# Reordering and splitting in a linear-attention and gated-MLP kernel: half-size crossbar transposes, a fifth output buffer, maxima split on VectorE, the tail's projection per batch, more tasks a step

## The chip, the cores and the metric

The kernel runs on one core of a Trainium2 chip. The metric is the device time of one execution in microseconds (us). Before the change the first three runs took 294.79, 297.31 and 300.43 us; with a fourth run beside the changed kernel the median is 296.06 us. Engines: PE is TensorE (PEld its weight loads), DVE is VectorE, ACT is ScalarE, POOL is GpSimd, SP is SyncE, which here only issues DMAs. Runs are called fast or slow by their time against the fastest of the same kernel. The profile of before was taken in a run of 301.7 us, state slow; that of the changed kernel in a run of 311.41 us, state fast.

## The reference

Two stages. The first is attention with a feature map for 8 batches, 8 heads, 576 tokens, head size 64; the second is a gated MLP that mixes tokens.

```python
def phi(x):
    proj = einsum('bhsd,df->bhsf', x, w_phi)
    proj = proj - max(abs(proj), axis=-1, keepdims=True)
    return concatenate([exp(proj), exp(-proj)], axis=-1)
q_p, k_p = phi(q), phi(k)
kv  = einsum('bhsf,bhsd->bhfd', k_p, v);   z = sum(k_p, axis=2)
out = einsum('bhsf,bhfd->bhsd', q_p, kv) / (einsum('bhsf,bhf->bhs', q_p, z)[..., None] + 1e-6)
x = out with heads side by side                        # 8 x 576 x 512
h = maximum(x @ w_in, 0);  u, v = halves of h          # 512 columns each
v_n = (v - mean(v)) / sqrt(var(v) + 1e-6)
v_s = einsum('ts,bsd->btd', w_spatial, v_n) + b_spatial
y = (u * v_s) @ w_out
```

## The kernel before

576 tokens are four blocks of 128 and a tail of 64. The attention runs in units: 32 units of two heads of one batch (four a batch), and four tail units, which each hold the 64-token tails of two batches. Each loop step starts the projections of one unit, while older units are in later phases. The second stage of a batch is a list of tasks: v (a projection, whose rows are normalised on GpSimd, `vn`), u (the other half), s (mixing of tokens, reads `vn`), o (the last matrix). Each step hands out tasks from a queue against a credit.

```python
def cross(b):                                    # both transposes of a whole batch, two steps ahead
    d = st[b]
    for x in ("k", "q"):
        d[x + "T"] = ld.tile([P, 2 * H, P], BF16, tag=x + "T_b", name=x + "T_b", bufs=2)
        pin(nc.sync.dma_start_transpose)(out=d[x + "T"], in_=d[x].rearrange("p h x -> p (h x)"))

def r_queries(u):                                # maxima of the queries, in two bf16 parts
    m, early = mhl[u["i"] % NM], u["i"] < EARLY
    pq = u["pq"]
    mq = pq[0][:, 0, 0:H] if early else small.tile([P, H], FP32, tag="mq", name="mq")
    for par in range(2):
        nc.vector.tensor_reduce(out=mq[:, 4 * par:4 * par + 4], in_=pq[par], axis=AX.X, op=ALU.max,
                                apply_absolute_value=True)
    eng = nc.vector if early else nc.gpsimd      # ... the split itself
    # [cut]
    eng.tensor_copy(out=m[:, :, 0:4], in_=mq)
    eng.tensor_tensor(out=m[:, :, 4:8], in0=mq, in1=m[:, :, 0:4], op=ALU.subtract)

def b_tasks(b):
    g, bl = b // 2, b % 2
    alone = g in SPLIT                           # SPLIT = (0,): batches 0 and 1 are done singly
    bls = [bl] if alone else [0, 1]
    tail = alone or bl == 1
    ts = []
    if tail: ts.append((mm, lambda: b_v_tail(g, bls)))
    ts += [(mm, lambda j=j: b_v(b, j)) for j in range(NB)]
    ts.append((0.0, lambda: b_ln(b)))            # normalises v of this batch on GpSimd
    # [cut]
    ts += [(mm, lambda dc=dc: b_u(b, dc)) for dc in range(KC)]
    if tail:                                     # s and o of BOTH batches of the pair
        ts.append((mm * len(bls) / 2, lambda: b_u_tail(g, bls)))
        for x in bls: ts += [(ms, lambda dc=dc, x=x: b_s(2 * g + x, dc)) for dc in range(KC)]
        ts.append((ms * len(bls) / 2, lambda: b_s_tail(g, bls)))
        for x in bls: ts += [(mm, lambda j=j, x=x: b_o(2 * g + x, j)) for j in range(NB)]
        ts.insert(len(ts) - 2, (mm, lambda: b_o_tail(g, bls)))
    return ts

RATE = 3.35                                      # us of tasks a step
def fill(share):                                 # called four times a step
    credit[0] = min(credit[0] + RATE * share, CAP)
    while queue and credit[0] >= queue[0][0] / 2:
        cost, task = queue.pop(0); task(); credit[0] -= cost
```

`a_scale` of a tail unit scales the tail's values for both batches on GpSimd (`vst`); `tail_num` and `tail_x_t` are the tail's attention and its transposes. The chain from the maxima is DVE (maxima), GpSimd (split `mhl`; VectorE before unit 5), PE (a transpose), DVE (copy to `mT`), PE (features `pf` of the next step). PE's instructions are kept in program order from step 8 on, so a PE wait holds all later work.

Of the kernel before, what the change touches and what calls it, by code (L numbers as in the profile page):

```python
# [16 lines left out]
def kernel(  # L17
# [15 lines left out]
    nc = tc.nc  # L33
# [39 lines left out]
    def pin(start):  # L73
        return lambda *a, **kw: tc.keep_in_program_order(start(*a, **kw))
# [40 lines left out]
        for i in range(2):  # L115
            pin(eng.dma_start)(out=gs[g][x][i * TL:(i + 1) * TL], in_=tail_ap(t, 2 * g + i))

    def cross(b):
        d = st[b]
        for x in ("k", "q"):  # L120
            d[x + "T"] = ld.tile([P, 2 * H, P], BF16, tag=x + "T_b", name=x + "T_b", bufs=2)
            pin(nc.sync.dma_start_transpose)(out=d[x + "T"], in_=d[x].rearrange("p h x -> p (h x)"))


    wphi_f = cpool.tile([P, F], FP32)
# [2 lines left out]
    alloc(0)  # L128
    first = {}
    for x, t in (("k", k), ("q", q)):  # L130
        first[x] = s2.tile([P, 2, NB * D], FP32, tag="ob", name="first", bufs=4)
        pin(nc.sync.dma_start)(out=first[x], in_=main_ap(t, 0, 0, 2))
    ident = cpool.tile([P, P], BF16)
    make_identity(nc, ident)
# [46 lines left out]
    w_out_bf = cpool.tile([P, KC, DM], BF16)  # L181
    wsp = s2.tile([P, NB, T0], BF16, tag="vn", name="wsp", bufs=2)
    wspr = cpool.tile([P, NB, TL], BF16)
    wspt = ld.tile([TL, S], BF16, tag="kT_b", name="wspt", bufs=2)
    bsp_row = ld.tile([P, S], FP32, tag="qT_b", name="bsp_row", bufs=2)
    nc.sync.dma_start(out=bsp_row[TL:TL + 1, :], in_=moe_b_spatial)
    nc.sync.dma_start(out=bsp_row[0:1, :], in_=moe_b_spatial)

# [35 lines left out]

    def a_transpose(u):
        src = st[u["b"]] if u["pair"] else gs[u["g"]]
        if "kT" in src:
            for x in ("kT", "qT"):
                u[x] = src[x][:, 4 * u["pj"]:4 * u["pj"] + 4, :] if u["pair"] else src[x]
            return  # L230
        for x, copy in (("k", nc.vector.tensor_copy if u["i"] < EK else nc.scalar.copy), ("q", nc.vector.tensor_copy)):
            pt = psum.tile([P, 4, P], BF16, tag="bank", name="pt")
            for j in range(4):
                if u["pair"]:
                    blk = src[x][:, 2 * u["pj"] + j // 2, (j % 2) * P:(j % 2 + 1) * P]
                else:
                    blk = src[x][:, 2 * j:2 * j + 2, :]
                transpose(out=pt[:, j, :], in_=blk, identity=ident)
            u[x + "T"] = a1.tile([P, 4, P], BF16, tag=x + "T", name=x + "T", bufs=2 if x == "k" else 4)
            copy(out=u[x + "T"], in_=pt)  # L240
# [51 lines left out]
                                 bias=0.0, scale=sc)  # L292

    def r_queries(u):
        m, early = mhl[u["i"] % NM], u["i"] < EARLY
        pq = u["pq"]
        mq = pq[0][:, 0, 0:H] if early else small.tile([P, H], FP32, tag="mq", name="mq")
        for par in range(2):
            nc.vector.tensor_reduce(out=mq[:, 4 * par:4 * par + 4], in_=pq[par], axis=AX.X, op=ALU.max,  # L299
                                    apply_absolute_value=True)  # L300
        eng = nc.vector if early else nc.gpsimd
        m = m.rearrange("p (par n) -> p par n", par=2)
        mq = mq.rearrange("p (par n) -> p par n", par=2)
        eng.tensor_copy(out=m[:, :, 0:4], in_=mq)
        eng.tensor_tensor(out=m[:, :, 4:8], in0=mq, in1=m[:, :, 0:4], op=ALU.subtract)

    def a_scale(u):
        em = small.tile([P, 2, H], FP32, tag="em" if u["pair"] else "em_t", name="em", bufs=3 if u["pair"] else 1)
# [146 lines left out]
    def b_v_tail(g, bls):  # L455
        d = gs[g]
        r = slice(bls[0] * TL, (bls[-1] + 1) * TL)
        vr = s2.tile([P, HALF], BF16, tag="vr", name="vr", bufs=5)
        stats = small.tile([P, 6], FP32, tag="stats", name="stats")
        mv = small.tile([P, 1, 2], FP32, tag="mv_t", name="mv_t")  # L460
        v_mm(lambda kc: d["xTt"][:, kc, r], vr, r, stats, mv[:, 0, :])
        rstd = root(mv, r, 1)
        for bl in bls:
            r = slice(bl * TL, (bl + 1) * TL)
            normalize(vnt[g % 2][r, bl, :], vr[r], rstd[r, 0, :])

    def b_u(b, dc):
        d = st[b]
        pu = psum.tile([P, T0], FP32, tag="bank", name="pu")
        for kc in range(KC):  # L470
            matmul(out=pu, lhsT=w_in_bf[:, kc, dc * P:(dc + 1) * P], rhs=d["xT"][:, kc, :],
                             start=(kc == 0), stop=(kc == KC - 1))
        nc.scalar.activation(out=d["uT"][:, dc, :], in_=pu, func=AF.Relu, bias=0.0, scale=1.0)
# [38 lines left out]
    def o_mm(lhs, r):  # L512
        po = psum.tile([P, DM], FP32, tag="bank", name="po")
        for dc in range(KC):
            matmul(out=po[r], lhsT=lhs(dc), rhs=w_out_bf[:, dc, :], start=(dc == 0), stop=(dc == KC - 1))
        ob = s2.tile([P, DM], FP32, tag="ob", name="ob", bufs=4)
        (nc.scalar.copy if drain[0] else nc.vector.tensor_copy)(out=ob[r], in_=po[r])  # L517
        return ob

# [30 lines left out]
    def b_tasks(b):  # L550

        g, bl = b // 2, b % 2
        alone = g in SPLIT
        bls = [bl] if alone else [0, 1]
        tail = alone or bl == 1
        mm = KC * T0 / 2400.0
        ms = (KC + 1) * T0 / 2400.0
        ts = []
        if tail:
            ts.append((mm, lambda: b_v_tail(g, bls)))  # L560
        ts += [(mm, lambda j=j: b_v(b, j)) for j in range(NB)]
        ts.append((0.0, lambda: b_ln(b)))
        if b == 0:
            ts += [(0.3, lambda i=i: transpose_spatial(i)) for i in range(NB + 1)]
        ts += [(mm, lambda dc=dc: b_u(b, dc)) for dc in range(KC)]
        if tail:
            ts.append((mm * len(bls) / 2, lambda: b_u_tail(g, bls)))
            for x in bls:
                ts += [(ms, lambda dc=dc, x=x: b_s(2 * g + x, dc)) for dc in range(KC)]
            ts.append((ms * len(bls) / 2, lambda: b_s_tail(g, bls)))  # L570
            for x in bls:
                ts += [(mm, lambda j=j, x=x: b_o(2 * g + x, j)) for j in range(NB)]
            ts.insert(len(ts) - 2, (mm, lambda: b_o_tail(g, bls)))
        return ts

    RATE = 3.35
    CAP = 2.5
    LAGS = dict(next=-1, maxima=1, features=2, sums=2, attention=3, out=4)
    FIRST = dict(next=-1, maxima=1, features=2, sums=2, attention=3, out=3)
# [58 lines left out]
            run("maxima", a_max_t)  # L638

    def finish_batch(u, f):  # L640
        g, bl = u["g"], u["b"] % 2
        if g in SPLIT:
            f(g, [bl])
        elif bl == 1:
            f(g, [0, 1])


    AT, AB, XP = 4, 5, 2
# [2 lines left out]
    def at(i, f, *a):  # L651
        io.setdefault(i, []).append(lambda: f(*a))
# [11 lines left out]
    for u in units:  # L664
        if not u["pair"] and u["g"] > 0:
            at(u["i"] - AT, load_tail, "k", u["g"])
            at(u["i"] - AT + 1, load_tail, "q", u["g"])
            at(u["i"] - AT + 1, load_tail, "v", u["g"])
        if u["pair"] and u["pj"] == 0 and u["b"] > 1:
            at(u["i"] - AB, load, "k", u["b"])  # L670
            at(u["i"] - AB + 1, load, "q", u["b"])
            at(u["i"] - AB + 1, load_v, u["b"], nc.sync)
            if u["b"] >= XB:
                at(u["i"] - XP, cross, u["b"])
    for i in range(NU + 4):
        step(i)
        for f in io.get(i, []):
# [34 lines left out]
```

## Time and profile before

| | before |
|---|---|
| median of 4 runs | 296.06 us |
| span of the profiled run (state slow) | 299.8 us |
| busy PE / DVE / ACT / POOL | 253.3 / 216.9 / 215.3 / 180.4 us |
| start of step 8 to start of step 35 | 50.9 to 240.7 us |
| last matmul | 295.2 us |

I cut the trace by steps: a step is the stretch from one unit's first key matmul (pk) on PE to that of the next. The windows view gives the busy time of each engine (us, number of instructions) in a stretch; here the steps 8 to 34 of the kernel before, and what follows:

```profile
50.90:240.70 189.80, 166.01 (x2286) 102.52 (x2284) 147.62 (x357) 151.80 (x358) 126.90 (x233) 0.96 0.87 136
240.70:295.20 54.50, 54.42 (x512) 29.42 (x508) 31.91 (x73) 24.79 (x47) 15.64 (x29) 1.00 0.22 75
```

The order is PE, PEld, DVE, ACT, POOL, then the granted clock, the DMA share and GB/s. In the first stretch PE, DVE and ACT are all within 43 us of the full 189.8; in the second PE alone is full. The prediction below shows the waits.

### The profile page before, as it was taken

The page shows a single profiled execution, that of the slowest core. Times are in us where ns is not written, and L with a number is a line of the kernel's source. Part 1 is how long each engine was busy: PE and PEld are TensorE (multiplying, and loading weights), DVE is VectorE, ACT ScalarE, POOL GpSimd, SP SyncE. Part 2 cuts the span into 40 slices and gives each one's busy share as a digit, 9 for nine tenths or more (in the row PEclk, how much of TensorE's full clock was granted, in tenths as well). Part 3 has the DMA queues.
Part 4 walks back from the last instruction along what each step waited for, and adds up shares of the span by engine and source line. Part 5 has one row for each costly group of instructions (what it writes and reads, how often), then busy time and mean ns, then how long its engine had stood idle before and what let it go on. Part 6 is the DMA issues. An engine that isn't in the chain of part 4 may idle for free.

```text
span 299.8 us, 8368 instructions
## 1 busy us (share of the span) xinstructions
PE 253.3 (84%) x3270; PEld 155.7 (52%) x3270; DVE 216.9 (72%) x538; ACT 215.3 (72%) x488; POOL 180.4 (60%) x320
## 2 busy tenths in 40 slices
PE   3059988989897989869699999819999999999993
PEld 1037666666553546535456567414555656645451
DVE  6277998877998569678686899819779787855520
ACT  7547999898589778839998888607999965067033
POOL 8239988589436696365959973923398850038400
PEclk9999999999999899979899999978999999999998
DMA  7979999942869199979941999899910011520026
GB/s 178 212 145 130 209 241 200 160 142 33 115 179 137 40 204 143 152 208 224 134 97 37 203 150 127 215 281 224 144 21 18 20 20 65 175 81 2 0 105 210
DMA packets 81706, 40.32 MB, mean 134 GB/s; under 512 B 50242, under 2 KB 77058, under 8 KB 81668
## 3 DMA queue, kind: packets, MB, share of 16 engines
q1 hardware_dynamic: 54180, 28.32, 43.4%
q0 software_dynamic: 27328, 11.41, 35.0%
q8 instruction: 25, 0.41, 0.5%
q14 instruction: 13, 0.11, 0.1%
q10 hardware_dynamic: 160, 0.07, 0.1%
HBM read 32.85 MB, written 9.44 MB: 141 GB/s over the span
## 4 chain that ended last, share of the span: by engine, by line
PE 50%; ACT 19%; DMA 10%; DVE 9%; POOL 7%; issue 3%; SPq 0%; DVEq 0%; POOLq 0%; ACTq 0%
PE ps L62 11%; PE pv L62 10%; ACT qf L277 10%; PE po L62 9%; PE pf L62 5%; ACT kf L291 5%; PE pu L62 5%; DMA out_dram<-ob 4%; DMA q_tl<-in_q_dram 4%; PE pn L62 3%; PE pt L62 3%; DVE stats L421 2%; POOL vn L435 2%; DMA qT_b<-q_bf 2%; PE pk L62 2%
## 5 line engine op out<-in xcount | busy, mean ns | idle before, releaser
L277 ACT ACTIVATE qf<-pf 128x512 bf16<-128x512 f32 x144 | 75.2, 631 | 32.8 <-PE pf L62 32.8
L315 POOL TENSOR_TENSOR vs<-v_f,em 128x512 bf16<-128x512 f32 x64 | 65.9, 1043 | 36.9 <-ACT em L310 30.8
L291 ACT ACTIVATE kf<-pk 128x512 bf16<-128x512 f32 x144 | 79.4, 664 | 8.4 <-DVE mk L286 8.3
L286 DVE TENSOR_REDUCE mk<-pk 128x4 f32<-128x512 f32 x72 | 46.4, 684 | 13.0 <-PE pk L62 12.4
L299 DVE TENSOR_REDUCE mq<-pq 128x4 f32<-128x512 f32 x62 | 40.7, 681 | 0.3 <-PE pq L62 0.3
L62 PE MATMUL ps<-w_spT,vn 128*128 128x512 bf16 (+1 forms) x256 | 38.8, 287 | 1.7 <-POOL vn L435 0.9
L421 DVE BATCH_NORM_STATS2 stats<-vr 128x6 f32<-128x512 bf16 (+1 forms) x37 | 25.0, 685 | 11.2 <-ACT vr L420 11.2
L62 PE MATMUL pv<-w_in_bf,xT 128*128 128x512 bf16 x128 | 33.0, 398 | 0.0
L62 PE MATMUL pu<-xT,w_in_bf 128*128 128x512 bf16 x128 | 32.0, 385 | 0.7 <-DVE mq L299 0.5
L495 DVE TENSOR_TENSOR uT<-ps,uT 128x512 bf16<-128x512 f32 x32 | 22.0, 687 | 14.6 <-PE ps L62 12.7
L420 ACT ACTIVATE vr<-pv 128x512 bf16<-128x512 f32 (+1 forms) x37 | 22.7, 654 | 13.1 <-PE pv L62 12.8
L62 PE MATMUL po<-w_out_bf,uT 128*128 128x512 bf16 x128 | 32.0, 388 | 0.0
L62 PE MATMUL pv<-vs,kf 128*128 128x66 bf16 x512 | 26.1, 200 | 3.3 <-DVE ob L517 3.3
L517 DVE COPY ob<-po 128x512 f32<-128x512 f32 (+1 forms) x28 | 19.0, 686 | 13.5 <-DMA out_dram<-ob 10.4
L62 PEld LDWEIGHTS <-qf 128*128 128x128 bf16 (+1 forms) x640 | 23.8, 101 | 9.7 <-issue 2.4
L62 PEld LDWEIGHTS <-kf 128*128 128x128 bf16 x640 | 24.7, 101 | 7.7 <-issue 4.9
L62 PE MATMUL pn<-kv,qf 128*128 128x66 bf16 (+1 forms) x640 | 26.0, 195 | 2.1 <-ACT qf L277 1.9
L62 PE MATMUL pf<-mT,sel 64*128 64x128 bf16 x288 | 16.9, 232 | 11.5 <-DVE mT L337 10.6
L360 DVE TENSOR_TENSOR x<-pn,rc 128x256 bf16<-128x256 f32 x64 | 24.9, 417 | 0.3
L330 POOL TENSOR_TENSOR vst<-v_tl,em 64x512 bf16<-64x512 f32 x16 | 16.4, 1038 | 13.9 <-ACT em L310 13.7
L435 POOL TENSOR_SCALAR vn<-vr,rs 128x512 bf16<-128x512 bf16 x32 | 24.2, 768 | 0.7
L62 PEld LDWEIGHTS <-vn 128*128 128x128 bf16 x256 | 16.2, 98 | 13.9 <-POOL vn L435 1.8
(106 smaller groups left out, 450.1 us busy)
## 6 DMA issues: line engine op xcount, KB each, us to landing
v_f<-in_v_dram SPq DMA_DIRECT2D x8, 1024.0 KB, 10.5
out_dram<-ob SPq DMA_DIRECT2D x32, 256.0 KB, 2.5
k_bf<-in_k_dram POOLq DMA_DIRECT2D x7, 512.0 KB, 7.1
q_bf<-in_q_dram POOLq DMA_DIRECT2D x7, 512.0 KB, 7.8
v_tl<-in_v_dram SPq DMA_DIRECT2D x8, 128.0 KB, 6.5
w_in_bf<-in_moe_w_in_dram POOLq DMA_DIRECT2D x2, 512.0 KB, 7.9
out_dram<-ob SPq DMA_DIRECT2D x8, 128.0 KB, 2.4
k_tl<-in_k_dram POOLq DMA_DIRECT2D x8, 64.0 KB, 6.0
```

Source lines behind the costliest of these rows:

```text
L62: r = f(*a, **kw)
L277: nc.scalar.activation(out=qf[:, s, 4 * par:4 * par + 4, :], in_=u["pf"][par], func=AF.Exp, bias=0.0, scale=sc)
L286: nc.vector.tensor_reduce(out=mk[:, par, :], in_=u["pk"][par], axis=AX.X, op=ALU.max, apply_absolute_value=True)
L291: nc.scalar.activation(out=u["kf"][:, s, 4 * par:4 * par + 4, :], in_=u["pk"][par], func=AF.Exp, bias=0.0, scale=sc)
L299: nc.vector.tensor_reduce(out=mq[:, 4 * par:4 * par + 4], in_=pq[par], axis=AX.X, op=ALU.max, apply_absolute_value=True)
L315: nc.gpsimd.tensor_tensor(out=vs[:, s, :, 0:D], in0=st[u["b"]]["v"][:, pj * H:(pj + 1) * H, :], in1=em[:, s, :].unsqueeze(2).to_broadcast( ...
L360: nc.vector.tensor_tensor(out=x, in0=pn[r, :, 0:D], in1=rc[r].to_broadcast([n, 4, D]), op=ALU.mult)
L420: nc.scalar.activation(out=dst[r], in_=pv[r], func=AF.Relu, bias=0.0, scale=1.0)
L421: nc.vector.bn_stats(out=stats[r], in_=dst[r])
L435: nc.gpsimd.tensor_scalar(out=dst, in0=src, scalar1=rs[:, 0:1], scalar2=rs[:, 1:2], op0=ALU.mult, op1=ALU.add)
L495: nc.vector.tensor_tensor(out=d["uT"][:, dc, :], in0=ps, in1=d["uT"][:, dc, :], op=ALU.mult)
L517: (nc.scalar.copy if drain[0] else nc.vector.tensor_copy)(out=ob[r], in_=po[r])
```

## The change

The intent: take away PE's waits for DMAs and for output buffers, take the hop to GpSimd out of the maxima's chain, finish each batch before the next one comes, and leave less work for the end, where only PE is busy.

```diff
-    def cross(b):
+    def cross(b, x, part):                      # half a tensor at a time
+        t = ld.tile([P, H, P], BF16, tag=x + "T_b", name=x + "T_b", bufs=4)
+        st[b].setdefault(x + "T", {})[part] = t
+        pin(nc.sync.dma_start_transpose)(out=t, in_=st[b][x][:, 4 * part:4 * part + 4].rearrange("p h x -> p (h x)"))
 ...
-        mq = pq[0][:, 0, 0:H] if early else small.tile([P, H], FP32, tag="mq", name="mq")
+        mq = pq[0][:, 0, 0:H]                   # always in PSUM
 ...
-        eng.tensor_copy(...); eng.tensor_tensor(...)       # GpSimd from unit 5 on
+        nc.vector.tensor_copy(...); nc.vector.tensor_tensor(...)
 ...
-        ob = s2.tile([P, DM], FP32, tag="ob", name="ob", bufs=4)
+        ob = s2.tile([P, DM], FP32, tag="ob", name="ob", bufs=5)
 ...  in b_tasks
-        if tail:
-            ts.append((mm, lambda: b_v_tail(g, bls)))
+        ts = [(mm, lambda: b_v_tail(g, [bl]))]
 ...
-            for x in bls:
-                ts += [(ms, lambda dc=dc, x=x: b_s(2 * g + x, dc)) for dc in range(KC)]
+        ts += [(ms, lambda dc=dc: b_s(b, dc)) for dc in range(KC)]
 ...  (o likewise)
-    RATE = 3.35
+    RATE = 3.75
 ...  in finish_batch (the tail's attention and transposes)
-        if g in SPLIT: f(g, [bl])
-        elif bl == 1: f(g, [0, 1])
+        f(u["g"], [u["b"] % 2])
 ...  when the transposes are issued
-                at(u["i"] - XP, cross, u["b"])
+                for n, (x, part) in enumerate((("k", 0), ("q", 0), ("k", 1), ("q", 1))):
+                    at(u["i"] - XP - 1 + n, cross, u["b"], x, part)
```

More of the change, by code (lines that the diff above doesn't have):

```diff
@@ L116, in load_tail @@
             pin(eng.dma_start)(out=gs[g][x][i * TL:(i + 1) * TL], in_=tail_ap(t, 2 * g + i))
-    def cross(b):
-        d = st[b]
-        for x in ("k", "q"):
-            d[x + "T"] = ld.tile([P, 2 * H, P], BF16, tag=x + "T_b", name=x + "T_b", bufs=2)
-            pin(nc.sync.dma_start_transpose)(out=d[x + "T"], in_=d[x].rearrange("p h x -> p (h x)"))
+    def cross(b, x, part):
+        t = ld.tile([P, H, P], BF16, tag=x + "T_b", name=x + "T_b", bufs=4)
+        st[b].setdefault(x + "T", {})[part] = t
+        pin(nc.sync.dma_start_transpose)(out=t, in_=st[b][x][:, 4 * part:4 * part + 4].rearrange("p h x -> p (h x)"))
     wphi_f = cpool.tile([P, F], FP32)
@@ L130 @@
     for x, t in (("k", k), ("q", q)):
-        first[x] = s2.tile([P, 2, NB * D], FP32, tag="ob", name="first", bufs=4)
+        first[x] = s2.tile([P, 2, NB * D], FP32, tag="ob", name="first", bufs=5)
         pin(nc.sync.dma_start)(out=first[x], in_=main_ap(t, 0, 0, 2))
@@ L183 @@
     wspr = cpool.tile([P, NB, TL], BF16)
-    wspt = ld.tile([TL, S], BF16, tag="kT_b", name="wspt", bufs=2)
-    bsp_row = ld.tile([P, S], FP32, tag="qT_b", name="bsp_row", bufs=2)
+    wspt = ld.tile([TL, S], BF16, tag="kT_b", name="wspt", bufs=4)
+    bsp_row = s2.tile([P, S], FP32, tag="uT", name="bsp_row", bufs=2)
     nc.sync.dma_start(out=bsp_row[TL:TL + 1, :], in_=moe_b_spatial)
@@ L226, in a_transpose @@
         src = st[u["b"]] if u["pair"] else gs[u["g"]]
-        if "kT" in src:
+        if u["pair"] and u["b"] >= XB:
+            y = u["pj"] % 2
             for x in ("kT", "qT"):
-                u[x] = src[x][:, 4 * u["pj"]:4 * u["pj"] + 4, :] if u["pair"] else src[x]
+                u[x] = src[x][u["pj"] // 2][:, 4 * y:4 * y + 4, :]
             return
@@ L294, in r_queries @@
     def r_queries(u):
-        m, early = mhl[u["i"] % NM], u["i"] < EARLY
-        pq = u["pq"]
-        mq = pq[0][:, 0, 0:H] if early else small.tile([P, H], FP32, tag="mq", name="mq")
+        m, pq = mhl[u["i"] % NM], u["pq"]
+        mq = pq[0][:, 0, 0:H]
         for par in range(2):
@@ L300, in r_queries @@
                                     apply_absolute_value=True)
-        eng = nc.vector if early else nc.gpsimd
         m = m.rearrange("p (par n) -> p par n", par=2)
         mq = mq.rearrange("p (par n) -> p par n", par=2)
-        eng.tensor_copy(out=m[:, :, 0:4], in_=mq)
-        eng.tensor_tensor(out=m[:, :, 4:8], in0=mq, in1=m[:, :, 0:4], op=ALU.subtract)
+        nc.vector.tensor_copy(out=m[:, :, 0:4], in_=mq)
+        nc.vector.tensor_tensor(out=m[:, :, 4:8], in0=mq, in1=m[:, :, 0:4], op=ALU.subtract)
     def a_scale(u):
@@ L552, in b_tasks @@
         g, bl = b // 2, b % 2
-        alone = g in SPLIT
-        bls = [bl] if alone else [0, 1]
-        tail = alone or bl == 1
         mm = KC * T0 / 2400.0
         ms = (KC + 1) * T0 / 2400.0
-        ts = []
-        if tail:
-            ts.append((mm, lambda: b_v_tail(g, bls)))
+        ts = [(mm, lambda: b_v_tail(g, [bl]))]
         ts += [(mm, lambda j=j: b_v(b, j)) for j in range(NB)]
@@ L565, in b_tasks @@
         ts += [(mm, lambda dc=dc: b_u(b, dc)) for dc in range(KC)]
+        tail = g in SPLIT or bl == 1
+        bls = [bl] if g in SPLIT else [0, 1]
         if tail:
             ts.append((mm * len(bls) / 2, lambda: b_u_tail(g, bls)))
-            for x in bls:
-                ts += [(ms, lambda dc=dc, x=x: b_s(2 * g + x, dc)) for dc in range(KC)]
+        ts += [(ms, lambda dc=dc: b_s(b, dc)) for dc in range(KC)]
+        if tail:
             ts.append((ms * len(bls) / 2, lambda: b_s_tail(g, bls)))
-            for x in bls:
-                ts += [(mm, lambda j=j, x=x: b_o(2 * g + x, j)) for j in range(NB)]
+        ts += [(mm, lambda j=j: b_o(b, j)) for j in range(NB)]
+        if tail:
             ts.insert(len(ts) - 2, (mm, lambda: b_o_tail(g, bls)))
         return ts
-    RATE = 3.35
+    RATE = 3.75
     CAP = 2.5
@@ L640, in finish_batch @@
     def finish_batch(u, f):
-        g, bl = u["g"], u["b"] % 2
-        if g in SPLIT:
-            f(g, [bl])
-        elif bl == 1:
-            f(g, [0, 1])
+        f(u["g"], [u["b"] % 2])
     AT, AB, XP = 4, 5, 2
```

## The prediction

> **What bounds the kernel now.** I began with the engine totals and the slices, because they say whether one engine is full.
>
> ```profile
> PE 253.3 (84%) x3270; PEld 155.7 (52%) x3270; DVE 216.9 (72%) x538; ACT 215.3 (72%) x488; POOL 180.4 (60%) x320
> ...
> PE   3059988989897989869699999819999999999993
> ...
> PEclk9999999999999899979899999978999999999998
> ```
>
> No engine is full, but PE is at 9 in most slices, with holes at slices 17, 19, 20 and 26 (1 is the hole near 195 to 202 us), and the granted clock drops in the same places (digits 8, 7, 8, 7, 8). [...]I cut the trace by steps, a step being the stretch from one unit's first key matmul (pk) to the next one's. A dense step: step 25, 170.6 to 176.2 us, 5.6 us, holds three s tasks (5 matmuls of 512 columns each; the chain shows such a task at 1.08 us), so the attention work of a step alone costs PE 5.6 - 3.2 = 2.4 us. Steps 8 to 35 start at 50.9 us and end at 246.4 us: 195.5 us for 28 steps. Counting which tasks the queue hands out there (a task of v, u or o is 4 matmuls, 0.86 us in the chain), they hold 91 us of tasks. PE needs 28 x 2.4 + 91 = 158 us; about 37 us are lost. The waits of PE say where:
>
> ```profile
> PE pf L62 <- DVE mT L337: 10.6, 8, 6.2
> ...
> PE pv L62 <- DVE ob L517: 3.3, 1, 3.3
> ...
> PE pt L62 <- POOL mhl L305: 2.0, 1, 2.0
> ...
> PE pq L62 <- DMA qT_b<-q_bf: 1.8, 2, 1.2
> ...
> PE pk L62 <- DMA kT_b<-k_bf: 0.9, 1, 0.9
> ```
>
> (who waits, for whom, us in total, times, longest.) The largest, 6.2 us, is put down to the copy mT, but the timeline of DVE shows its real cause:
>
> ```profile
> 200.23 0.69 DVE L517 COPY ob<-po 128x512 f32<-128x512 f32 x1 [5.83 <-DMA out_dram<-ob]
> 200.84 0.22 DVE L337 COPY mT<-pt 128x128 bf16<-128x128 bf16 x1
> ```
>
> DVE stood for 5.83 us for a free output buffer, in front of the mT copy that PE needed. The output store of that time took 8.12 us in the chain, against a median of 2.5 us, because the 1 MB load of v and the loads of k and q were running. The 3.3 us wait is the same thing with another cause, in the queue of SP:
>
> ```profile
> 116.31 6.54 SPq L74 DMA_TRANSPOSE kT_b<-k_bf  x1
> 123.39 3.14 SPq L74 DMA_TRANSPOSE qT_b<-q_bf  x1
> 126.62 1.00 SPq L523 DMA_DIRECT2D out_dram<-ob  x2
> ```
>
> The whole-batch transposes held SP for 6.54 and 3.14 us, and two finished outputs were issued only after them. Last, the end. The chain in order of time:
>
> ```profile
> 261.61 3.45 PE pv L62 x16
> 265.51 3.45 PE pu L62 x16
> 268.97 4.32 PE pv L62 x20
> 273.29 4.35 PE pu L62 x32
> 277.63 9.80 PE ps L62 x80
> 287.43 7.79 PE po L62 x36
> ```
>
> For 33.7 us PE alone sets the pace, with nothing of attention beside it: nearly all of the work of batches 6 and 7 was still queued.
>
> **What the Trainium skill says.** "TensorE: Matmul & The Clock Gate", section "HAM oscillation": PE idle for more than about 3.4 us falls back to half clock, which then also taxes the work after the gap. The trace agrees in substance: the windows 96 to 99.4, 130 to 133.4, 147 to 150.4 and 198.4 to 205.2 us had a granted clock of 0.51, 0.51, 0.52 and 0.50, and each follows a PE wait (for kT_b and qT_b, ob, mhl, ob); some of these waits were shorter than 3.4 us. So a removed wait also gives back part of a slow window. "DMA: Bandwidth & Descriptors", section "Issuing engines are not separate DMA queues": DMAs from all issuers interleave on the same 16 engines; the 8.12 us store agrees. "Perfetto Trace Analysis", section "Identifying the Most-Contended Engine": PE busy is a poor measure; the 2.4 us per step above is why I agree.
>
> **The change part by part.** From the order of instructions on each engine: PE gains 24 matmuls, DVE 87 instructions (540 to 627), POOL loses 50, SP's transposes of k and q go from 12 to 24, each half as large.
>
> *More tasks a step (3.35 to 3.75 us), and s and o per batch.* Replaying the queue: before, batches 2, 4 and 6 only got v and u, and their s and o waited for the odd batch; 29.2 us of tasks were left at the end. After, every batch is finished before the next arrives, and 18.1 us are left (batch 7 alone). From the chain: of 33.2 us, the first 3.45 was handed out before the end, 29.7 remain; after: 4.32 + 4.35 + 4.3 + 1.2 (half of ps, and the tail) + 7.79 x 5/9 = 18.5 us. The end gets 11.2 us shorter. But s of batch 7 now directly follows its u: from the last v, one relu 0.65, statistics 0.68 + 0.18, root 0.24 + 0.87 + 0.2 + 0.25, four normalisations 0.77 each = 6.1 us, covered by u 4.35 and the first s matmuls 0.65: +1 to +2 us. The last steps 36 to 39 carry 15.4 instead of 13.4 us: +2. Net -7.5 us after step 35.
>
> Steps 8 to 35 then carry 103 instead of 91 us of tasks: PE needs 67 + 103 = 170 us (the extra projections are in it: three more, of 4 x 0.216 us). This fits in the old 195.5 only if losses shrink.
>
> *Fifth output buffer.* A batch with its tail makes at most five outputs, so with five buffers DVE need not wait inside a batch. Takes away 6.2 + 3.3 us of PE waits.
>
> *Transposes in halves.* k's first half is issued three steps ahead instead of two, SP is held half as long at a time. Takes away most of 1.8 + 0.9 us and of the cause of the 3.3. DMA work is the same.
>
> *Maxima on DVE.* 31 x (0.155 + 0.158) = 9.7 us more on DVE, 12.2 us less on POOL (6.0 + 6.2). Removes the hop to POOL and its queueing behind a 1.04 us vs: the wait of 2.0 us, once, and some of the 0.5 us ones.
>
> *Tail's projection per batch.* +3 statistics, +6 pairs of reciprocal and product, +3 copies: 2.5 + 3.5 + 1.1 = 7 us on DVE; +1.7 on ACT; +4.7 on POOL (3 roots).
>
> *DVE in all:* 216.9 + 9.7 + 7 + 4 outputs more (ACT drains fewer, 2.7) = 236 us. In steps 8 to 39 some 190 of 216: no bound, but close.
>
> The sum for steps 8 to 35. Of the 37 lost, 14 go with the waits named, 5 with half clock (17 us at half, 5 of them idle anyway), 3 with the empty queue of steps 20 and 21 (5.3 us each for 3.3 and 2.4 us of PE work): 15 stay. New: steps with five v and a u (ACT 5.0 for the eight exponentials and the small ones + 6 x 0.62 = 8.7 against PE 7.5): before, two such steps took 8.7 and 8.9 us, now six, +5; steps with one or two tasks (12, 17, 26, 35), which can't fall under about 5.2 us of ACT, +4; waits for vn, of which the chain shows 3.03 us of normalising ahead of an s near 105 us, +3. 170 + 15 + 12 = 197. Adding instead the steps one by one, from before's steps of like content (8.8 for v, 6.9 for u, 6.7 for s, 5.3 to 6.3 for o), gives 193. I take 195, as long as before.
>
> So the gain is about 7.5 us at the end, and from the rest 0 +- 5; I lean a little to the good side, since a lost clock is the least certain cost. 297.3 - 9 = 288.
>
> **Rivals.** (1) *DVE becomes the bound.* For: an s step needs about 3.9 + 3 x 0.69 there and the mT copy sits behind it; before, eight waits on mT are in the list. Against: 190 of 216 us. Then the loop grows by 5 to 8 us and the time is about 295. (2) *PE stays full and throttling vanishes.* For: each slow window follows a gap that the change removes. Then losses fall to 12 to 15, the loop is 184 us, the time about 278 to 280. (3) *The waits only move*: five v in one step pile up on ACT, POOL must do two roots and five normalisations at once, s waits for vn in each batch: 2 us x 6, about 292 to 296. (4) *The outputs are hidden anyway*: against, the 5.83 us wait of DVE held PE for 6.2.
>
> **Range and chances.** The end is nearly arithmetic (-6 to -9); the loop may be -9 to +6. This gives 281 to 296 for 8 in 10, with 288 in the middle. The runs before span 294.8 to 300.4, so 2% is about 291: faster 0.62, within 0.34, slower 0.04.
>
> **What would show it.** Right: the last stretch of PE alone is near 21 us, no DVE wait for out_dram over 1 us, no PE wait for POOL mhl, no DMA wait for kT_b or qT_b, steps 8 to 35 near 195 us, DVE busy near 236. Wrong: slices with PE under 7 after a v step or ahead of s (vn, rival 3), waits of pf for mT growing over 10 us (rival 1), or a loop near 184 us at full clock (rival 2).

## The result

The changed kernel took 311.2 us (median of 4 runs, 309.18 to 314.26), against 296.06 us before. The ratio is 1.0504 (95% interval 1.040 to 1.061): slower by 5%. A ratio is the mean time of one kernel's fast runs over that of the other's fast runs of the same rounds, so it is not quite the ratio of the medians. The output is correct.

The page of the changed kernel, engine totals and slices:

```profile
PE 255.8 (83%) x3251; PEld 157.4 (51%) x3294; DVE 231.6 (75%) x625; ACT 215.1 (69%) x487; POOL 174.4 (56%) x270
...
PE   3279789898997988878887999869797998998983
...
PEclk9999999999997999997999999997999999999999
```

The deep hole at slice 26 (counted from 0) is gone, but the row has many 7s and 8s in place of the 9s, about one dip every few slices, and PE is no longer full near the end. The clock has only three dips left, so a lower clock alone does not explain the loss. The windows, for the same stretches (start of step 8 to start of step 35, and what follows):

```profile
48.90:254.80 205.90, 178.67 (x2369) 110.76 (x2403) 166.44 (x441) 153.80 (x360) 121.58 (x186) 0.98 0.79 132
254.80:304.60 49.80, 45.19 (x410) 24.10 (x412) 27.32 (x70) 22.51 (x44) 15.74 (x29) 1.00 0.16 54
```

The end became 4.7 us shorter, the steps 16.1 us longer. (The profile of before is of a slow run and that of the changed kernel of a fast one, so between fast runs the steps should have grown by no less.) DVE's busy time in the steps went from 147.6 to 166.4 us. The waits of PE (who, for whom, us in total, times, longest):

```profile
PE pf L62 <- DVE mT L335: 13.5, 12, 1.8
PE ps L62 <- POOL vn L433: 6.2, 13, 1.2
```

The named DMA waits are gone from this list: none for kT_b, qT_b or the maxima on GpSimd, and DVE's list has none for the output store. In their place stand twelve waits for mT, none over 1.8 us, and thirteen for vn, which were 0.9 us in total before.

Where the vn waits come from is seen in step 19, 132.1 to 141.9 us. First PE's timeline (start, duration, what, and in brackets the idle time before it and its releaser), then POOL's:

```profile
132.09 0.40 PE L62 MATMUL pk<-wphi,kT_b 64*128 64x128 bf16 x8
...
138.37 0.39 PE L62 MATMUL ps<-w_spT,vn 128*128 128x512 bf16 x1 [1.22 <-POOL vn L433]
139.12 0.39 PE L62 MATMUL ps<-w_spT,vn 128*128 128x512 bf16 x1 [0.37 <-POOL vn L433]
...
140.63 0.39 PE L62 MATMUL ps<-w_spT,vn 128*128 128x512 bf16 x1 [0.36 <-POOL vn L433]
...
141.87 0.64 PE L62 MATMUL pk<-wphi,kT_b 64*128 64x128 bf16 x8
```

```profile
130.80 2.04 POOL L328 TENSOR_TENSOR vst<-v_tl,em 64x512 bf16<-64x512 f32 x2
...
133.10 2.05 POOL L328 TENSOR_TENSOR vst<-v_tl,em 64x512 bf16<-64x512 f32 x2
...
137.54 3.03 POOL L433 TENSOR_SCALAR vn<-vr,rs 128x512 bf16<-128x512 bf16 x4
```

The s task that stands right behind its own u runs at the pace of GpSimd, one matmul for each block that is normalised. GpSimd started late because it first did the two scalings of the tail (vst, 4.5 us from 130.80 to 135.35), which nobody needs before step 21; the root for this batch (135.44 to 137.43 us) came only after them.

The waits for mT are seen at the end of step 20, on DVE:

```profile
148.37 0.43 DVE L358 TENSOR_TENSOR xt<-pn,rc 64x256 bf16<-64x256 f32 x1
...
148.93 0.69 DVE L493 TENSOR_TENSOR uT<-ps,uT 128x512 bf16<-128x512 f32 x1
149.65 0.43 DVE L358 TENSOR_TENSOR xt<-pn,rc 64x256 bf16<-64x256 f32 x1
150.11 0.23 DVE L335 COPY mT<-pt 128x128 bf16<-128x128 bf16 x1
```

and on PE:

```profile
150.39 0.40 PE L62 MATMUL pf<-mT,sel 64*128 64x128 bf16 x8 [1.26 <-DVE mT L335]
```

The tail's attention (xt) and a product of s stand in front of mT, and PE waits for them. The tail's attention of this odd batch stood in step 20 of the kernel before too, where PE waited 0.70 us for mT; new beside it here are three products of s (uT), where the queue gave one task of u before. So two theories came out of the trace: that the place of s and o is what costs (ORDER), or the denser steps (RATE). A third was that the maxima on VectorE lie on the path (MAXIMA); a fourth, that the doubled work of the tail does (WORK).

### The profile page after: what moved, and what is told of

It is laid out like the page before. It is cut to its first block, busy times and chain, and to the rows that moved or that the text cites. A ratio compares the mean times of both kernels' runs of the same rounds, so it can differ in the third digit from the quotient of the medians.

```text
span 309.5 us, 8463 instructions
## 1 busy us (share of the span) xinstructions
PE 255.8 (83%) x3251; PEld 157.4 (51%) x3294; DVE 231.6 (75%) x625; ACT 215.1 (69%) x487; POOL 174.4 (56%) x270
## 4 chain that ended last, share of the span: by engine, by line
PE 28%; DVE 26%; ACT 25%; POOL 8%; issue 7%; DMA 3%; POOLq 0%; DVEq 0%; ACTq 0%; another core or an unknown queue 0%
ACT qf L277 13%; ACT kf L291 9%; PE ps L62 8%; DVE stats L419 7%; PE pf L62 7%; DMA q_tl<-in_q_dram 3%; DVE x L358 3%; POOL vn L433 3%; DVE pq L298 3%; PE pu L62 3%; PE po L62 3%; PE pv L62 3%; DVE mk L286 3%; DVE ob L515 2%; DVE uT L493 2%
## 5 line engine op out<-in xcount | busy, mean ns | idle before, releaser
L298 DVE TENSOR_REDUCE pq<-pq 128x4 f32<-128x512 f32 x72 | 49.9, 693 | 1.5
L62 PE MATMUL ps<-w_spT,vn 128*128 128x64 bf16 (+1 forms) x244 | 40.6, 288 | 7.8 <-POOL vn L433 6.2
L419 DVE BATCH_NORM_STATS2 stats<-vr 128x6 f32<-128x512 bf16 (+1 forms) x40 | 26.9, 680 | 9.2 <-ACT vr L418 9.0
L62 PE MATMUL po<-w_out_bf,uT 128*128 128x512 bf16 x120 | 30.1, 380 | 1.9 <-ACT kf L291 0.9
L62 PEld LDWEIGHTS <-qf 128*128 128x128 bf16 (+1 forms) x640 | 25.9, 101 | 9.7 <-issue 1.5
L62 PE MATMUL pv<-w_in_bf,xT 128*128 128x512 bf16 x120 | 29.4, 379 | 0.6 <-issue 0.2
L62 PE MATMUL pn<-kv,qf 128*128 128x66 bf16 (+1 forms) x640 | 27.8, 196 | 1.8 <-ACT kf L291 0.8
L62 PE MATMUL pf<-mT,sel 64*128 64x128 bf16 x288 | 16.1, 225 | 14.8 <-DVE mT L335 13.5
L426 POOL TENSOR_SCALAR var<-mv_t 64x1 f32<-64x1 f32 x8 | 1.9, 239 | 44.3 <-DVE mv_t L420 30.7
L358 DVE TENSOR_TENSOR x<-pn,rc 128x256 bf16<-128x256 f32 x64 | 26.6, 420 | 0.4
L62 PEld LDWEIGHTS <-w_in_bf 128*128 128x128 bf16 x208 | 15.4, 99 | 14.2 <-issue 3.4
```

The lines of the kernel that those rows point to most:

```text
L62: r = f(*a, **kw)
L358: nc.vector.tensor_tensor(out=x, in0=pn[r, :, 0:D], in1=rc[r].to_broadcast([n, 4, D]), op=ALU.mult)
L419: nc.vector.bn_stats(out=stats[r], in_=dst[r])
```

## The experiments

Fourteen more kernels ran, each at least 3 rounds beside the kernel before (4 to 20 runs, the profiled one among them). The medians of before were 297.52 (first four), 296.56 (next four), 297.44 (next four) and 297.64 us (last two; two of its runs there, of 409.43 and 822.7 us, count as slow and enter no ratio). Different calls ran on different chips, so I compare ratios, and treat differences under about 0.01 between calls as no more than hints. By the 2% rule of the verdicts f, b, g and j are slower than before, d, h and l unclear, and c, e, k, m, n, p and r the same; where I speak of smaller differences, they rest on the intervals. All outputs were correct.

### Undo the order of tasks: c_after_paired

The changed kernel with the old lists of tasks and the old `finish_batch`; RATE stays 3.75.

```diff
-        ts = [(mm, lambda: b_v_tail(g, [bl]))]            # and s, o of this batch
+        if tail: ts.append((mm, lambda: b_v_tail(g, bls)))  # and s, o of both, as before
-        f(u["g"], [u["b"] % 2])
+        if g in SPLIT: f(g, [bl])
+        elif bl == 1: f(g, [0, 1])
```

> The changed kernel with the old order of second-stage tasks: even batches get v and u only, and s, o, the tail's projection and the tail's attention come once per pair of batches; everything else (halves, five output buffers, maxima on VectorE, 3.75) as changed. Theory ORDER (s follows its own u, so PE waits for the normalisation on GpSimd, and the tail's extra work falls into every batch): the loss goes, 290 to 297 us, PE waits for vn under 2 us. Theory RATE (3.75 us of tasks a step is more than ScalarE and VectorE can drain): stays at 305 us or more. Theory MAXIMA (0.3 us more on VectorE a step delays mT): 304 to 310 us.

296.5 us, ratio 0.9985 (0.994 to 1.003). The loss of 5% against before goes with this one part, as theory ORDER had it; no PE wait for vn is left in the list. Theory RATE falls, at least in its plain form: 3.75 us a step in the old order does not make the kernel slower than before. It could still eat up some of the gain of the halves and the fifth buffer; e_halves_ob5_dve below tests that.

### Only what takes waits away: d_halves_ob5

The kernel before with the transposes in halves and five output buffers, nothing else.

> The kernel before with only the transposes in halves and the fifth output buffer; old maxima, old order, 3.35. All theories: these take waits away, so 285 to 292 us, no VectorE wait for an output store over 1 us. If it is 295 or more, the removed waits did not lie on the path, or others took their place.

290.96 us, ratio 0.9755 (0.968 to 0.983). Expected by all and met: these two parts are a gain of 2.5% (2.2% by the medians of the call, 290.96 against 297.52). No DVE wait for a store is in its list. It is the fastest kernel of the study in its ratio.

### The maxima back on GpSimd: f_after_poolmax

```diff
-        mq = pq[0][:, 0, 0:H]
+        mq = pq[0][:, 0, 0:H] if early else small.tile([P, H], FP32, tag="mq", name="mq")
+        eng = nc.vector if early else nc.gpsimd           # and the split on eng
```

> The changed kernel with the splitting of the maxima back on GpSimd (from step 5 on). Theory MAXIMA: most of the loss goes, 300 us or less, and PE's waits for mT fall under 8 us. Theories ORDER and RATE: 308 to 315 us, rather worse, as GpSimd is the engine that PE waits for.

308.0 us, ratio 1.0326 (1.025 to 1.041) against 1.0504. Neither text was right: the maxima are not most of the loss, but moving them to VectorE cost, it did not help, even in this kernel where GpSimd is late for vn. PE's waits for mT did not fall (13.9 us in 17 waits), so with the maxima in PSUM total waits on mT are not how the cost shows; see k_e_sbuf below.

### Fewer tasks a step: b_after335

```diff
-    RATE = 3.75
+    RATE = 3.35
```

> The changed kernel with 3.35 us of tasks a step instead of 3.75. Theory RATE: most of the loss goes, 296 to 300 us. Theory ORDER: little changes, 306 to 314 us: the steps get a little shorter but 27.5 instead of 18.1 us of tasks are left for the end, and s still follows its own u. Theory MAXIMA: the same as ORDER.

306.95 us, ratio 1.0301 (1.023 to 1.037). This lies in the range of ORDER, at its low edge, but about 2 of the 5% go. In the trace steps 8 to 34 take 188.1 us instead of 205.9, and what follows grows from 54.7 to 66.0 us. The waits for mT fell (from 13.5 us), those for vn did not (from 6.2 us):

```profile
PE ps L62 <- POOL vn L433: 8.3, 16, 1.1
PE pf L62 <- DVE mT L335: 6.0, 7, 1.4
```

So in this order 3.75 us a step costs 2%, and the order still costs 3%.

### The maxima on VectorE alone: e_halves_ob5_dve

d_halves_ob5 with `r_queries` of the change.

> The kernel with halves and five output buffers of the first set (291.0 us), and the maxima split on VectorE; old order, 3.35. The paired order at 3.75 with these maxima gave 296.5. If the maxima cost what they cost in the changed kernel (308.0 against 311.2 us), this gives 293 to 296 us and the denser steps cost little in the old order; if they cost nothing here, 290 to 292, and then 3.75 is what costs 5 us in the old order.

295.39 us, ratio 0.9988 (0.996 to 1.002) against 0.9755: the maxima on VectorE take back what the first two parts had given, some 2.3% by the ratios (1.5% by the medians, 295.39 against 290.96, which are from two calls). And c_after_paired, which is this kernel with 3.75, has the same ratio (0.9985): with the maxima on VectorE the denser steps cost and give nothing in the old order.

The trace shows where a step without any DVE shortage gets longer. Step 23 was 5.77 us in d_halves_ob5 and is 6.28 us here. The two query maxima, first in d_halves_ob5, then here:

```profile
156.35 1.28 DVE L299 TENSOR_REDUCE mq<-pq 128x4 f32<-128x512 f32 x2
```

```profile
157.41 1.49 DVE L298 TENSOR_REDUCE pq<-pq 128x4 f32<-128x512 f32 x2
...
159.07 1.02 PE L62 MATMUL pu<-xT,w_in_bf 128*128 128x512 bf16 x3 [0.35 <-ACT kf L291]
```

Both maxima now write into one bank of the projections that they read. The pair takes 1.49 instead of 1.28 us, and a u task of the same step waits 0.35 us for ScalarE's kf, which it did not in the other kernel. I take it that the second maximum now waits for the first, and that u got a bank that is freed later because the maxima hold theirs until the split; no run shows that by itself.

### The maxima in SBUF: j_mq_sbuf and k_e_sbuf

To see whether PSUM is the cost, the maxima go to SBUF, with the split still on VectorE, in the changed kernel (j) and in e_halves_ob5_dve (k).

```diff
-        mq = pq[0][:, 0, 0:H]
+        mq = small.tile([P, H], FP32, tag="mq", name="mq")
```

> The changed kernel with the maxima written to SBUF instead of into the PSUM bank of the projections; VectorE still splits them. If what the maxima cost (some 3 us, as the run with them on GpSimd shows) comes from a PSUM bank held until the split is done, this gives 308 to 309 us; if it comes from VectorE's time, 310.5 to 312 us.

315.36 us, ratio 1.0651 (1.058 to 1.073): worse by 1.5%, which no text had. The steps of u do get their old length back (step 23: 5.76 us), but PE waits 18.5 us for mT in 18 waits instead of 13.5 in 12. In the old order:

> Halves, five buffers and the maxima split on VectorE in the old order (ratio 0.999 to the kernel before, against 0.976 with GpSimd), but the maxima written to SBUF instead of PSUM. In the changed kernel SBUF was 4 us worse than PSUM. If that holds in general: 298 to 301 us. If it was an accident of the order of VectorE's instructions there: 290 to 296.

294.12 us, ratio 0.9911 (0.988 to 0.994), better than PSUM (0.9988), and still 1.6% short of GpSimd (0.9755). So the sign of PSUM against SBUF depends on the order around it; I call that an accident of the order, and did not find the instruction that decides it. What holds in all four pairs is that the split on VectorE costs against GpSimd: 0.9988 and 0.9911 against 0.9755, 1.0504 and 1.0651 against 1.0326. (The intervals of 1.0504 and 1.0326 just touch; a fifth pair, g_defer_scale at 1.0319 against r_poolmax_defer at 1.0044 below, is clear.)

The waits for mT tell the two places apart. In the old order, with the maxima on GpSimd (d), on VectorE in PSUM (e) and on VectorE in SBUF (k):

```profile
PE pf L62 <- DVE mT L337: 7.6, 10, 2.0
PE pf L62 <- DVE mT L335: 7.3, 9, 1.6
PE pf L62 <- DVE mT L335: 12.8, 14, 2.0
```

In the changed kernel the three are 13.9, 13.5 and 18.5 us. So with SBUF the cost shows as waits for mT, some 5 us more in both orders; with PSUM it does not, and the longer steps of u are the place where I see it.

### One order swapped on GpSimd: g_defer_scale

In the changed kernel, the tail's scalings are emitted after the normalisation and both are kept in program order. The traces show the instructions of PE, VectorE and ScalarE in the same order as before the swap; only GpSimd's differ.

```diff
-            for bl in range(2 if u["i"] > 1 else 1): tail_scale(u["g"], bl)
+            if u["i"] == 1: tail_scale(u["g"], 0)
 ...
+            at(u["i"], tail_scale, u["g"], 0); at(u["i"], tail_scale, u["g"], 1)
 ...   pin() around the three instructions of tail_scale and around normalize
```

> The changed kernel with one order swapped on GpSimd: the two scalings of a tail's values (vst, 4.6 us) come after the normalisation of the batch whose s is next, instead of before it. TensorE, VectorE and ScalarE keep their instructions in the same order. Theory ORDER, part vn (s waits for GpSimd): steps 19 and 28, 9.8 and 9.9 us long, fall to 7 to 7.5 us, in all 306 to 307.5 us, PE waits for vn under 4 us instead of 6.2. If the tail's extra work on VectorE is all of the loss: 310 to 312.

305.98 us, ratio 1.0319 (1.025 to 1.038). Steps 19 and 28 went from 9.78 and 9.94 to 6.52 us each, and PE's waits for vn from 6.2 to 1.6 us; the theory of the order had 7 to 7.5 us and under 4 us. GpSimd now does:

```profile
137.70 3.02 POOL L74 TENSOR_SCALAR vn<-vr,rs 128x512 bf16<-128x512 bf16 x4
140.69 2.04 POOL L74 TENSOR_TENSOR vst<-v_tl,em 64x512 bf16<-64x512 f32 x2
...
142.99 2.04 POOL L74 TENSOR_TENSOR vst<-v_tl,em 64x512 bf16<-64x512 f32 x2
```

So the order of two jobs on GpSimd, in two places of the kernel, cost 1.85% of the time, some 5.5 us. In the profiled run of the changed kernel two of the three stretches at half clock (141.3 to 144.7 and 209.6 to 213.0 us, granted clock 0.51 and 0.50) follow right on these waits, and here steps 19, 20, 28 and 29 have the full clock. But the mean clock of all runs here (0.969 to 0.986) is not above that of the changed kernel (0.982 to 0.992), so how much of the gain came through the clock stays open.

### The tail's work per batch, s and o in pairs: h_paired_tailwork and p_tailattn

h is c_after_paired with the tail's attention, transposes and value projection once per batch; p has only the attention and the transposes per batch.

```diff
 h and p:  f(u["g"], [u["b"] % 2])                        # finish_batch of the change
 h only:   ts.append((mm, lambda: b_v_tail(g, [bl])))     # in every batch
```

> The paired-order kernel of the first set (296.5 us) with the tail's work per batch: its attention, transposes and value projection once for each batch as in the change (24 matmuls and about 7 us of VectorE more), while s and o stay in pairs. Theory WORK (the doubled tail work is the loss): 304 us or more. Theory ORDER (where s and o stand is the loss): 297 to 301 us.

302.95 us, ratio 1.0231 (1.016 to 1.030). This lies between the two texts: the work costs 2.5%, and s and o per batch then cost 2.7% more (1.0504), the 1.85% of g_defer_scale among them.

> The paired-order kernel at 3.75 (ratio 0.999 to the kernel before) with only the tail's attention and its transposes once per batch; the tail's value projection stays once per pair. With both per batch the ratio was 1.023. If VectorE's extra reciprocals, products and copies (1 us each in the steps of even batches) are the loss: 1.015 to 1.025, 301 to 304 us. If the projection with its relu, statistics and root is: 1.000 to 1.008, 296 to 299 us.

300.25 us, ratio 1.0107 (1.007 to 1.015): half of the 2.5%, between the two texts. Step 25, in which the attention of batch 4, an even one, ends, shows it in the windows (start of step 25 to 179.4 us, the start of step 26 in both); first c_after_paired, then p_tailattn:

```profile
172.70:179.40 6.70, 6.65 (x84) 3.89 (x83) 6.10 (x16) 4.58 (x11) 5.47 (x8) 1.00 2.66 115
```

```profile
171.70:179.40 7.70, 7.39 (x103) 4.55 (x101) 7.01 (x20) 4.58 (x11) 5.25 (x8) 1.00 2.06 139
```

DVE has four instructions and 0.91 us more, and the step is 1.0 us longer. PE has 19 matmuls and 0.74 us more as well, so this view alone does not tell which of the two makes the step longer. PE's matmuls are taken from the odd batch's step (29), and that one got no shorter (8.0 and 8.3 us).

### Both repairs in the changed kernel: r_poolmax_defer

> The changed kernel with both repairs: maxima split on GpSimd (alone 1.033) and the tail's scalings after the normalisation (alone 1.032); the changed kernel itself 1.050. If the two losses are separate they add: 1.050 - 0.017 - 0.018 = 1.015, 300 to 303 us. If GpSimd's time is what PE waits for, the maxima on it eat the other gain: 1.025 to 1.033, 304 to 307 us.

298.1 us, ratio 1.0044 (1.000 to 1.008), better than the sum of the two, which neither text had. So undoing these two takes back 4.6 points; against d_halves_ob5 the changed kernel had lost 7.5. The 2.9 that remain (2.5 by the medians, 298.1 and 290.96) are the order per batch, the tail's work and the 3.75 us a step together: d has 3.35, and what 3.75 costs with the maxima on GpSimd was not run.

### Which of the two parts gained: m_halves_only and n_ob5_only

> The kernel before with the transposes in halves alone, four output buffers. Both together gave a ratio of 0.976. If the whole-batch transposes in front of the output stores were the cause of the waits, this has nearly all of it: 289 to 292 us. If the number of buffers was: 294 to 297, with a VectorE wait for an output store of some us left.

295.36 us, ratio 0.9886 (0.984 to 0.993), as expected if the number of buffers was the cause. DVE still waits for stores:

```profile
DVE ob L517 <- DMA out_dram<-ob: 5.4, 3, 2.9
```

> The kernel before with the fifth output buffer alone. If the buffers were the cause: 289 to 292 us. If the transposes were: 294 to 297 us; waits for kT_b and qT_b (2.7 us) and the slow clock after them stay in any case, so I expect about 293.

293.15 us, ratio 0.9863 (0.982 to 0.991), the 293 that was expected. One wait for a store is left (its profile is of a slow run):

```profile
DVE ob L517 <- DMA out_dram<-ob: 2.7, 1, 2.7
```

So five buffers alone did not end these waits, as the prediction had it; five buffers with the halves did. The two gains, 1.1 and 1.4%, add up to the 2.5% of both, within their intervals.

### More tasks a step on the best kernel: l_d_rate355

d_halves_ob5 with RATE 3.55.

> The best kernel so far (halves and five buffers, maxima on GpSimd, old order; ratio 0.976) with 3.55 us of tasks a step instead of 3.35. If the attention steps still have idle time on TensorE that a few more tasks can use, 286 to 289 us; if the steps only get longer by what the end gets shorter, 290 to 293 us, as 3.75 against 3.35 in the old order with the maxima on VectorE changed nothing (0.9985 and 0.9988).

291.67 us, ratio 0.9864 (0.981 to 0.991). No gain over 0.9755; whether it is a loss I can't say, since the two ran in different calls and the medians are 0.7 us apart. The trace shows where the tasks went. Start of step 8 to start of step 35, and what follows, first d_halves_ob5, then this one:

```profile
52.10:230.70 178.60, 160.34 (x2252) 101.19 (x2283) 146.90 (x357) 151.45 (x358) 127.10 (x232) 0.97 0.91 144
230.70:285.20 54.50, 53.90 (x504) 29.45 (x508) 31.94 (x73) 24.80 (x47) 15.71 (x29) 1.00 0.22 76
```

```profile
50.00:231.20 181.20, 163.31 (x2295) 101.84 (x2293) 147.94 (x359) 152.60 (x358) 126.62 (x230) 0.98 0.87 142
231.20:284.10 52.90, 52.27 (x502) 28.41 (x498) 30.55 (x71) 24.91 (x47) 16.17 (x31) 1.00 0.23 78
```

The end is 1.6 us shorter and the steps are 2.6 us longer. PE's busy time fell by 1.6 us in the one and rose by 3.0 in the other; work moved from the end to the steps cost at least as much there.

## Why the prediction was wrong

The prediction said 288 us, 281 to 296, and gave slower by over 2% a chance of 0.04. It was 311.2. The runs build the change up part by part; the ratio to the kernel before after each part:

| kernel | ratio | this part |
|---|---|---|
| halves and fifth buffer (d_halves_ob5) | 0.9755 | -2.5% |
| + maxima on VectorE (e_halves_ob5_dve) | 0.9988 | +2.3% |
| + 3.75 us a step (c_after_paired) | 0.9985 | 0.0% |
| + tail's attention per batch (p_tailattn) | 1.0107 | +1.2% |
| + tail's value projection per batch (h_paired_tailwork) | 1.0231 | +1.2% |
| + s and o per batch (the change) | 1.0504 | +2.7% |

Each ratio has an interval of some 0.003 to 0.010 on either side, and neighbours are mostly from different calls, so a part of 1.2% is little more than a hint. Nor are the parts independent: from 3.35 to 3.75 us a step costs 2.0% in the changed order (b_after335) and 0.0% in the old.

By its own steps:

- **Halves and the fifth buffer: right in kind, too large in size.** The prediction counted 12 us of waits (6.2, 3.3, 1.8 and 0.9) and 5 us of slow clock as taken away. The waits did go, but the runs show 2.5%, about 7 us. The profile of before was from a slow run of 301.7 us, so its list of waits may be on the long side for a fast run of some 296. Some waits came in their place (for vn 2.3 us in d_halves_ob5, before 0.9); where the rest went is not shown. The prediction also read a hole at slice 20, where the row has a 9, and placed the clock's dips at the holes; they stand at slices 13, 17, 19, 26 and 27, and at 13 and 27 PE has a 9.

- **Maxima on VectorE: wrong in sign.** The prediction booked 9.7 us more on DVE as lying beside PE's work and 2.0 us of waiting as a gain. The runs show 2.3% in the old order with PSUM, 1.6% with SBUF, and 1.8% in the changed kernel: 5 to 7 us, all loss. DVE was at 147.6 of 189.8 us busy in the steps, which looks like room. But the maxima come in each step, in front of the copy mT that the next step of PE needs. With SBUF the waits for mT did grow (7.6 to 12.8 us, 13.9 to 18.5). With PSUM they did not, and the steps of u grew instead (step 23, 5.77 to 6.28 us); why is argued above, not shown.

- **The tail's work per batch: mis-sized, as it was counted as beside.** The prediction had "7 us on DVE", 1.7 on ACT and 4.7 on POOL, and put none of it on the path except the three projections, 2.6 us of PE. It cost 2.5%, 7 us. Its attention alone, to which the prediction gave no time on the path, cost 1.2%; in step 25, with 0.91 us more of DVE and 0.74 us more of PE, the step was 1.0 us longer.

- **The sum for steps 8 to 35: this is the step that failed.** "I take 195, as long as before." It was 211.5. Steps 8 to 35, before and after:

```profile
50.90:246.40 195.50, 171.63 (x2363) 105.86 (x2359) 152.88 (x369) 156.27 (x369) 129.04 (x237) 0.96 0.84 133
48.90:260.40 211.50, 183.37 (x2445) 113.88 (x2478) 171.76 (x455) 158.28 (x371) 122.68 (x188) 0.98 0.79 134
```

PE's work grew as predicted, by 12 us (171.6 to 183.4 busy). What failed is the losses: of 37 us the prediction had 22 go and 12 come, 27 in all; by the same count 211.5 - 170 = 41.5 stood there. Of the adding of steps one by one, the v steps (8.8) came out at 8.8 to 9.5; the thin ones (5.3) at 5.1 to 5.6; these were about right. A u step was taken as 6.9 us: steps 19 and 28, right after a tail unit has started, took 9.8 and 9.9, with the waits for vn. An s step was taken as 6.7: steps 20 and 29 took 9.0 and 8.7, with the tail's attention and mT behind it. The steps with o of batches 1, 3 and 5 were taken as 6.3 and took 7.4 to 7.5 (16, 25, 34); the tail's attention of an even batch, which is new there, is in the same steps. These kinds of steps did not occur in the kernel before, so I had taken the length of the nearest thing that did.

- **The waits for vn: named, and too small.** The prediction's rival (3) named this wait and gave it 2 us a batch, 292 to 296 us; the sum had "+3". I had worked out the chain of one relu, statistics, root and normalisations, 6.1 us, without asking what GpSimd does in front of it. It did 4.5 us of scalings. Swapping them gave back 1.85%.

- **The end gets shorter: true and worth nothing.** The prediction's gain was 7.5 us after step 35; 4.7 us were measured from the start of step 35. A stall for vn before the last s was foreseen at 1 to 2 us; PE waited four times there, 1.4 us in all. The chain of the end shows it:

```profile
292.97 2.27 POOL vn L433 x3
...
295.28 2.98 PE ps L62 x13
```

But the error is deeper. The steps had no idle time of PE that the moved tasks could use: 0.9988 against 0.9985 for 3.35 and 3.75 in the old order, and 1.6 us less at the end for 2.6 us more in the steps in l_d_rate355. The prediction had the steps carry 12 us more of tasks in the same time, on the strength of waits that were to go; those waits gave 7 us, and other waits came.

- **Rival (1), DVE becomes the bound**, had 5 to 8 us for the loop, and its sign, the waits on mT over 10 us, was met (13.5). It was dismissed with "190 of 216 us". A busy share of 78% in the steps (147.6 of 189.8 us) did not clear an engine that stands in the chain of each step; that was the judgement at fault. Waits on mT are a poor measure of it, though: they are 11.5 us in r_poolmax_defer, which is as fast as before.

- **What was met.** PE alone at the end: 283.7 to 304.6 us, 20.9 us, against "near 21". No DVE wait for a store, no PE wait for the maxima on GpSimd, none for kT_b or qT_b. DVE busy 231.6 us against "near 236". Rival (4), that the outputs are hidden anyway, is refuted by d_halves_ob5 and n_ob5_only. Rival (2), a full PE and no slow clock, is refuted too: the granted clock rose from 0.967 (0.967 to 0.982 in fast runs of before in the next call) to 0.982 (0.992 at best) and the steps got longer all the same.

What stays open: what the order per batch still costs when GpSimd's order and the maxima are repaired (1.0044 against 0.9755); the tail's work would be 2.5 of these 2.9%, but the parts are from different calls and I did not run it without, nor 3.35 us a step with both repairs. And why SBUF for the maxima is better in one order and worse in the other.

## What to carry to other kernels

When two or three engines are each at about 80% in a pipelined loop, do not count an added instruction as free if it stands between a product of PE and what PE needs next, and do not credit the hole that it leaves on another engine: here 9.7 us of such instructions on VectorE cost 5 to 7 us. Moving work out of a tail where only one engine runs gave nothing here in the old order (0.9988 and 0.9985) and cost 2% in the changed one. When a consumer is moved closer to its producer, look at what else the producing engine has in its queue at that moment; here two jobs in the wrong order on GpSimd cost 5.5 us. The best kernel of this study keeps only the two parts that take a wait away and add no computing to any engine: 290.96 us.

## What the Trainium skill lacked or had wrong

- "TensorE: Matmul & The Clock Gate", section "HAM oscillation": its rule is that idle gaps of PE over some 3.4 us bring the half clock. Three of the four slow stretches that the prediction lists follow waits of 3.3 us or less each; the one from 147.0 to 150.4 us (granted clock 0.52) follows one of 1.96 us, with PE busy for 1.16 of the 3.4 us before it. In the changed kernel PE was busy for 1.84 of the 3.4 us before the one from 141.3 us, and no wait there was over 1.22 us. So the gap alone is no safe test. The next section of the page does say that frequent short idle times can do the same; it gives no share or length for that.
- "Perfetto Trace Analysis", section "Identifying the Most-Contended Engine": it calls occupancy of VectorE a fair measure of how close one is to roofline. Here VectorE was busy for 147.6 of 189.8 us (78%), and still 0.3 us more a step on it cost 1.6 to 2.3% of the kernel. The section does not say that distance from roofline is not room to spare in a chain.
- No page that I read has a figure for how long crossbar transposes of this size hold the queue that issues them. Whole-batch transposes of k held SP for a median of 4.1 us (2.0 to 7.5), halves for 1.3 us (1.2 to 2.3). Output stores behind them are issued that much later: in the lines of the prediction those of 126.62 us came after 6.54 and 3.14 us of transposes.
- No page that I read tells that a pair of VectorE reductions overlaps less when both write into a PSUM bank that one of them reads: the pair took 1.49 us, and 1.28 us with the results in SBUF (in k_e_sbuf too). A dependency between the two, which the program's order would then keep, is not excluded.
